# Turned steps spread over places, and side work placed by a table of engine load, in an attention and two-expert-layer kernel

## The chip, the cores and the metric

One core of a Trainium2 chip runs the whole program. The metric is the time on the device in microseconds (us). Three runs of the kernel before took 2199.93 to 2209.55, their median is 2204.12.

## The reference

Block-wise attention gives x (2304 tokens by 512); then comes a layer of 8 experts whose gates P are normalised over rows and columns 8 times; then an MLP with a gated activation.

```python
scores = scale * np.matmul(q_c, k_c.transpose(0, 1, 2, 4, 3))   # chunks of 64
attn = exp(scores - max) / (sum + 1e-09); out = np.matmul(attn, v_c)
...
for e in range(E):                       # 8 experts, 512 -> 1024 -> 512
    h = np.maximum(x @ w1[e], 0.0)
    out += P[:, e:e + 1] * (h @ w2[e])
...
h = x @ w_in                             # 512 -> 2048 -> 512
relu6 = np.clip(h + 3.0, 0.0, 6.0)
return ((h * relu6 / 6.0) @ w_out).astype(np.float32)
```

## The kernel before, in words

All matmuls of the layers work on pairs of operands, a high part in TensorE's reduced 32-bit type and a low part that is the rest: a product is high times high, high times low and low times high. ScalarE makes a high part (a copy), VectorE or GpSimd the low part (a subtraction); `cut_piece` (L789) does both.

The program goes through attention and the first expert (until about 306 us), and then through 108 **steps** (`slots`). A step is one of 36 sets of weights (28 of experts 1 to 7, 4 for each expert, and 8 of the MLP) times one third of the tokens (768). Six passes stand in a row: thirds 0, 1 and 2 with the 28 expert sets (steps 0 to 27, 28 to 55, 56 to 83), then thirds 0, 1 and 2 with the 8 MLP sets (84 to 107). From step 56 on they are called **turned**.

The first layer of a step is a block product with seven multiplications in place of eight (`ORDER`, `product`, L871): six matmuls of 128x384 for each, so 42 a step, into three banks of PSUM a, b and c. The order is 1 into a, 6 into b, 2 onto a, 7 onto b, 5 into c, 4 onto b, 3 onto c. Each of the seven is a **place** of the step. A product that goes onto a bank waits until the bank's first content has been read: ScalarE copies product 1 from a (p1, L916, ahead of product 2), VectorE adds the sums u2, u3 and p1 from b and c (L912).

- In a step of the first two passes `h_first` cuts four outputs, and the second layer of the step before (`mm2_chunk`, L993, 36 matmuls of 128x512) is put between the products.
- In a turned step `h_turned` makes gated outputs (`gate`: for an expert one VectorE instruction with the gate columns `pb`, L942; for the MLP a ScalarE relu, L948, and then a VectorE instruction, L949), and after product 3 four differences (L956) of them, each cut as it is made (`put`). These seven cut outputs are the operands of a second seven-product scheme: `second` takes two steps at a time, one output m of both (`MS` is their order), adds it to `accM` on VectorE (L1101; on ScalarE, L1099, for the first pair of a segment), and in the last pair of a segment adds the blocks to each other (`comb`, L1048, seven times).

Around this there is **side work**, put at (step, place) by `at_slot`: its instructions are issued behind those of the product of that place.

- Conversion (`cv_half`, L188 to L214): the MLP's weights come as 64-bit numbers and are turned into 32-bit ones with seven VectorE instructions for each of 32 pieces, four in one place and three two places later. All lie in the first pass.
- Weights of the expert sets: sums (`w1_sums` L775, `w2_sums` L786, four instructions in one place) and cuts, in the step or two before they are used; all operands are stored to be loaded again in later passes (`w1_load`, asked for two steps ahead).
- Weights of the MLP sets ahead of time (`w1_ahead`, `w2_ahead`): 8 sets in the second pass, 18 places for each; a half (w1 or w2) is cut in four pieces, the low part of w1's on VectorE, and stored whole (`wsc<-m`).
- The input of the MLP (`x2_cuts`): transposed at the end of a segment (`x2_T`), differences and seven cuts for each half.

Every queue runs in the order written; SyncE issues all loads and stores.

Of the kernel before, what the change touches and what calls it, by code (L numbers as in the profile page):

```python
# [9 lines left out]
F32 = mybir.dt.float32  # L10
F32R = mybir.dt.float32r
# [17 lines left out]
def chunk_attention_moe_mlp(  # L29
# [135 lines left out]
    cv_list = W_IN[:8] + W_OUT[:8] + W_IN[8:] + W_OUT[8:]  # L165
    cv_in = {}
    M = {}
# [5 lines left out]
    def cv_load(i):  # L173
        if i < len(cv_list):
            src, _, r, c = cv_list[i]
            t = part(i % 2 * 2 * CW, 2 * CW, U32)
            nc.sync.dma_start(
                out=t,
                in_=src.bitcast(U32)[r * 128:(r + 1) * 128, 2 * c * CW:2 * (c + 1) * CW],
            )  # L180
            cv_in[i] = t

    def cv_half(i, z):
        if z == 0:
            t = cv_in[i].rearrange("p (n a) -> p n a", a=2)
            hw = t[:, :, 1]
            kx = part(4 * CW + i % 2 * CW, CW, U32)
            nc.vector.tensor_scalar(  # L188
                out=kx, in0=hw, scalar1=20, scalar2=0x7FF,
                op0=ALU.logical_shift_right, op1=ALU.bitwise_and,  # L190
            )
            nc.vector.tensor_scalar(
                out=kx, in0=kx, scalar1=-896.0, scalar2=0.0, op0=ALU.add, op1=ALU.max
            )
            nc.vector.tensor_scalar(
                out=kx, in0=kx, scalar1=255.0, scalar2=8388608.0, op0=ALU.min, op1=ALU.mult
            )
            nc.vector.scalar_tensor_tensor(
                out=kx, in0=hw, scalar=0x80000000, in1=kx,
                op0=ALU.bitwise_and, op1=ALU.bitwise_or,  # L200
            )
            cv_in[i] = (t, kx)
            return
        t, kx = cv_in.pop(i)
        am = part(6 * CW, CW, U32)
        nc.vector.tensor_scalar(
            out=am, in0=t[:, :, 1], scalar1=0xFFFFF, scalar2=0x100000,
            op0=ALU.bitwise_and, op1=ALU.bitwise_or,
        )
        bt = part(7 * CW + i % 2 * CW, CW)  # L210
        nc.vector.scalar_tensor_tensor(
            out=bt, in0=t[:, :, 0], scalar=2.0 ** -32, in1=am, op0=ALU.mult, op1=ALU.add
        )
        nc.vector.scalar_tensor_tensor(  # L214
            out=bt, in0=bt, scalar=2.0 ** -20, in1=kx.bitcast(F32), op0=ALU.mult, op1=ALU.mult
        )
        cv_in[i] = bt
        cv_load(i + 2)

    def cv_keep(i):  # L220
        _, dst, r, c = cv_list[i]
        nc.sync.dma_start(
            out=dst[r * 128:(r + 1) * 128, c * CW:(c + 1) * CW], in_=cv_in.pop(i)
        )
# [469 lines left out]
    for seg, (p, mlp, ks) in enumerate(SEGS):  # L694
        for j, kset in enumerate(ks):
            slots.append(SimpleNamespace(
                i=len(slots), seg=seg, p=p, mlp=mlp, k=kset, e=1 + kset // NG4, q=kset % 2, j=j,
                turned=seg >= FIRST_TURNED, H={},
            ))
        ends.append(len(slots))  # L700
# [39 lines left out]
    raw1, raw2 = {}, {}  # L740

# [6 lines left out]

    def raw_load(k):
        s1, _, g = src_of(k)  # L750
        t = pools["raw1"].tile([128, 8, 2, 128], F32, tag="r1", name=f"r1_{k}")
# [7 lines left out]
    def raw_load2(k, ahead=False):  # L759
        _, s2, g = src_of(k)  # L760
        if ahead:
            t = pools["raw1"].tile([128, 8, 256], F32, tag="r1", name=f"r2_{k}")
        else:
            t = pools["raw2"].tile([128, 4, 256], F32, tag="r2", name=f"r2_{k}")
# [6 lines left out]
    def w1_sums(k):  # L771
        t = raw1[k]
        for o, x, y, op in ((4, 0, 1, ALU.add), (5, 4, 2, ALU.subtract), (6, 2, 0, ALU.subtract),
                            (7, 3, 5, ALU.subtract)):
            nc.vector.tensor_tensor(out=t[:, o], in0=t[:, x], in1=t[:, y], op=op)  # L775

    def w2_sums(k):
        r = raw2[k]
        if k < NEXP:
            t = pools["sum2"].tile([128, 4, 256], F32, tag="s2", name=f"s2_{k}")  # L780
        else:
            t = r[:, 4:8]
        A11, A12, A22, A21 = [r[:, o] for o in range(4)]
        for o, x, y, op in ((0, A21, A22, ALU.add), (1, t[:, 0], A11, ALU.subtract),
                            (2, A11, A21, ALU.subtract), (3, A12, t[:, 1], ALU.subtract)):
            nc.vector.tensor_tensor(out=t[:, o], in0=x, in1=y, op=op)  # L786
        raw2[k, "s"] = t
# [52 lines left out]
    def w1_ahead(k, z):  # L840
        w = part(0, 3584, F32R).rearrange("p (o a n) -> p o a n", o=7, a=2)
        if z < 4:
            o0, o1 = PIECES[z]
            r = raw1[k].rearrange("p o k f -> p o (k f)")[:, o0 + 1:o1 + 1]
            cut_ops(w, r, o0, o1, nc.vector)
            return
        raw1.pop(k)
        nc.sync.dma_start(
            out=wsc1[k].rearrange("o p n -> p o n"),
            in_=w.rearrange("p o a n -> p o (a n)").bitcast(F32),  # L850
        )

    def w2_ahead(k, z):
        w = part(0, 3584, F32R).rearrange("p (o a n) -> p o a n", o=7, a=2)
        if z < 4:
            o0, o1 = ((0, 2), (2, 4), (4, 6), (6, 7))[z]
            r = raw2[k, "s"][:, o0:o1] if z < 2 else raw2[k][:, o0 - 4:o1 - 4]
            cut_ops(w, r, o0, o1, nc.gpsimd)
            return
        raw2.pop(k), raw2.pop((k, "s"))  # L860
        w2_store(k, 0, w)
# [34 lines left out]
    def h_first(s, t, pr, ps, z):  # L896

        if pr == 1:
# [39 lines left out]

    def gate(s, out, src, nh):

        if not s.mlp:
            nc.vector.scalar_tensor_tensor(  # L942
                out=out, in0=src, scalar=0.0, in1=pb[s.p, s.e][:, nh * HN:(nh + 1) * HN],
                op0=ALU.max, op1=ALU.mult,
            )
            return
        u = temp(s, "u")
        nc.scalar.activation(out=u, in_=src, func=AF.Relu, bias=three)  # L948
        nc.vector.scalar_tensor_tensor(  # L949
            out=out, in0=u, scalar=6.0, in1=src, op0=ALU.min, op1=ALU.mult  # L950
        )

    def h_turned(s, t, pr, ps, z):

        first_sums(s, t, pr, ps)
        sub = lambda o, x, y: nc.vector.tensor_tensor(out=o, in0=x, in1=y, op=ALU.subtract)  # L956
        if pr == 2:
# [3 lines left out]
        elif pr == 5:  # L961
            gate(s, t["u3"], t["u3"], 1)
            put(s, 3, t["u3"])
        elif pr == 4:
            gate(s, t["p1"], t["p1"], 0)
            put(s, 2, t["p1"])
        elif pr == 3:
            t1, u2, u3, p1 = t["t1"], t["u2"], t["u3"], t["p1"]
            gate(s, u2, u2, 1)
            sub(t1, u2, t1)  # L970
            put(s, 5, t1)
            sub(u2, u3, u2)
            put(s, 7, u2)
            sub(u3, u3, t1)
            put(s, 6, u3)
            sub(p1, p1, u3)
            put(s, 4, p1)
# [41 lines left out]
    MS_LAST = (1, 6, 2, 7, 5, 3, 4)  # L1019
    COMB = {2: [(2, 1)], 5: [(3, 5)], 6: [(6, 1), (7, 6), (3, 6), (5, 7)], 4: [(4, 7)]}  # L1020
    DONE = {2: [2], 6: [3, 5], 4: [4]}
    COMB_LAST = {6: [(6, 1), (3, 6)], 2: [(2, 1)], 7: [(7, 6), (4, 7)], 5: [(3, 5), (5, 7)]}
    DONE_LAST = {2: [2], 5: [5], 3: [3], 4: [4]}
# [129 lines left out]
    def x2_diff(kl):  # L1153
        diffs(*x2t[kl])
# [42 lines left out]
    with tc.manual_schedule():  # L1197
# [140 lines left out]
        def to_right():  # L1338
# [4 lines left out]
            opened("r", "W10", 1, "right")  # L1343
            opened("rr", "raw1", 2, "right")
# [225 lines left out]
```

## Time and profile before

| | us |
|---|---|
| median of 3 runs | 2204.12 |
| the profiled execution | 2206.19 |
| its span, first to last instruction | 2204.3 |
| TensorE busy | 2004.4 |
| VectorE busy | 1425.6 |
| GpSimd busy | 1111.8 |
| ScalarE busy | 801.8 |

The granted clock of TensorE has a mean of 0.967 of full speed. PE is TensorE's matmuls, PEld its weight loads, DVE VectorE, ACT ScalarE, POOL GpSimd, SP SyncE. A busy time counts all of an engine's instructions, whether something waits for them or not; where time is lost is read from idle time and from what ended it.

### The profile page before, as it was taken

To read this page: it belongs to the slowest core of one execution; us is meant where nothing else is said; L and a number is where in the kernel's file an instruction comes from. 1 tells how busy PE (TensorE), PEld (TensorE's weight loads), DVE (VectorE), ACT (ScalarE), POOL (GpSimd) and SP (SyncE) were. 2 spreads that over 40 slices of the span, in tenths; PEclk is the share of its full clock that TensorE was granted. 3 is DMA by queue.
4 is the path that set the end of the run, shared out by engine and by line. 5 is a ranking of instruction groups with operands and counts; after the bars stand their busy time and mean duration, and the time that the engine had idled before them with its cause. 6 is when DMAs were issued, how large, how long until landed. Compare 5 with 4: busy or idle time off the path is not lost.

```text
span 2204.3 us, 33550 instructions
## 1 busy us (share of the span) xinstructions
PE 2004.4 (91%) x11709; PEld 1835.1 (83%) x11709; DVE 1425.6 (65%) x2310; ACT 801.8 (36%) x1586; POOL 1111.8 (50%) x965
## 2 busy tenths in 40 slices
PE   7999989999999999999989988999999877888887
PEld 6777777888888888887878878999999877888887
DVE  6555467787787655556655456777777757656666
ACT  3322234443344344444434423222222333343342
POOL 3213246676667566555555546554545445344343
PEclk9999999999999999999999999999999888999999
DMA  9756486686676779999989968777778777767663
GB/s 213 190 146 175 139 284 228 224 268 206 225 248 226 263 264 328 321 349 350 336 314 329 359 216 303 247 250 248 249 250 284 261 257 242 237 214 245 209 209 124
DMA packets 340935, 552.82 MB, mean 251 GB/s; under 512 B 46736, under 2 KB 170784, under 8 KB 340512
## 3 DMA queue, kind: packets, MB, share of 16 engines
q1 hardware_dynamic: 340768, 550.69, 75.5%
q8 instruction: 93, 1.52, 0.3%
q14 instruction: 74, 0.61, 0.1%
HBM read 365.97 MB, written 184.62 MB: 250 GB/s over the span
## 4 chain that ended last, share of the span: by engine, by line
PE 50%; DVE 25%; DMA 11%; ACT 5%; issue 5%; POOL 2%; SPq 1%; DVEq 0%; ACTq 0%; POOLq 0%
PE acc L993 11%; PE hb L871 9%; PE ha L871 7%; PE hc L871 6%; PE o L1089 5%; PE o L1080 3%; PE h L557 3%; DVE u L956 3%; PE acc L591 3%; DVE p L956 3%; DVE u L912 2%; DMA wsc<-SS 2%; ACT u L948 2%; DMA x2sc<-m 1%; DVE r L775 1%
## 5 line engine op out<-in xcount | busy, mean ns | idle before, releaser
L993 PE MATMUL acc<-W,H 128*128 128x512 f32 x2016 | 526.2, 396 | 5.1 <-POOL H L894 3.0
L993 PEld LDWEIGHTS acc<-W,H 128*128 128x128 f32 x2016 | 380.7, 191 | 66.0 <-POOL H L894 6.8
L871 PE MATMUL hb<-X,W 128*128 128x384 f32 x1560 | 326.5, 345 | 24.9 <-DVE u L912 24.8
L792 POOL TENSOR_TENSOR W<-r,W 128x512 fp32r<-128x512 f32 x220 | 291.8, 1349 | 56.7 <-ACT W L791 53.2
L871 PEld LDWEIGHTS hb<-X,W 128*128 128x128 f32 x1560 | 281.2, 193 | 42.0 <-DVE u L912 32.5
L871 PE MATMUL ha<-X,W 128*128 128x384 f32 x912 | 198.8, 355 | 88.6 <-ACT p L916 74.2
L871 PE MATMUL hc<-X,W 128*128 128x384 f32 x1200 | 245.1, 339 | 14.0 <-DVE H L888 9.8
L871 PEld LDWEIGHTS ha<-X,W 128*128 128x128 f32 x912 | 167.7, 198 | 102.9 <-ACT p L916 79.6
L894 POOL TENSOR_TENSOR H<-u,H 128x384 fp32r<-128x384 f32 x112 | 124.5, 1111 | 229.0 <-ACT H L893 199.9
L871 PEld LDWEIGHTS hc<-X,W 128*128 128x128 f32 x1200 | 212.6, 189 | 27.2 <-DVE H L888 13.5
L912 DVE TENSOR_TENSOR u<-hc,u 128x384 f32<-128x384 f32 x216 | 119.8, 555 | 146.2 <-PE hc L871 142.6
L912 DVE TENSOR_TENSOR u<-hb,p 128x384 f32<-128x384 f32 x216 | 119.7, 554 | 130.7 <-PE hb L871 106.1
L792 POOL TENSOR_TENSOR Hb<-u,Hb 128x384 fp32r<-128x384 f32 x108 | 125.0, 1168 | 126.3 <-ACT Hb L791 102.6
L892 ACT ACTIVATE u<-u 128x384 f32<-128x384 f32 x112 | 58.7, 524 | 292.9 <-DVE u L912 292.7
L1101 DVE SCALAR_TENSOR_TENSOR accM<-o,accM 128x768 f32<-128x768 f32 x154 | 146.1, 950 | 21.9 <-PE o L1089 12.1
L1080 PE MATMUL o<-W2R,Hb 128*128 128x256 f32 x882 | 144.5, 295 | 3.5 <-DVE accM L1101 3.3
L1089 PE MATMUL o<-Hb,W2R 128*128 128x384 f32 x672 | 145.9, 340 | 0.0
L1080 PEld LDWEIGHTS o<-W2R,Hb 128*128 128x128 f32 x882 | 132.2, 203 | 4.0 <-DVE accM L1101 3.5
L791 ACT ACTIVATE W<-r 128x512 fp32r<-128x512 f32 x224 | 122.8, 595 | 1.9 <-DMA r<-in_moe_w_dram 1.9
L1089 PEld LDWEIGHTS o<-Hb,W2R 128*128 128x128 f32 x672 | 121.3, 190 | 0.0
L792 POOL TENSOR_TENSOR Hb<-t,Hb 128x384 fp32r<-128x384 f32 x57 | 67.3, 1180 | 97.8 <-ACT Hb L791 91.2
L1089 PE MATMUL o<-Ha,W2R 128*128 128x384 f32 x504 | 110.8, 338 | 0.0
(190 smaller groups left out, 3585.5 us busy)
## 6 DMA issues: line engine op xcount, KB each, us to landing
W<-wsc SPq DMA_DIRECT2D x504, 256.0 KB, 4.1
W2R<-wsc SPq DMA_DIRECT2D x182, 512.0 KB, 4.3
wsc<-W SPq DMA_DIRECT2D x28, 1792.0 KB, 8.7
r<-in_moe_w_dram SPq DMA_DIRECT2D x112, 256.0 KB, 4.7
wsc<-SS SPq DMA_DIRECT2D x28, 1024.0 KB, 6.3
wsc<-m SPq DMA_DIRECT2D x16, 1792.0 KB, 8.7
wsc<-W SPq DMA_DIRECT2D x28, 768.0 KB, 5.9
x2sc<-m SPq DMA_DIRECT2D x42, 384.0 KB, 5.0
```

The lines of the kernel that those rows point to most:

```text
L557: nc.tensor.matmul(out=hps[:, :n], lhsT=w[:, a, kk, :], rhs=xx[:, kk, :], start=(kk == 0 and a == 0 and xx is xh), stop=(kk == KD - 1 and ...
L591: nc.tensor.matmul(out=o[:, :n] if turned else o, lhsT=w[:, a, c] if turned else hx[:, c], rhs=hx[:, :n] if turned else w[:, a, :], start= ...
L791: nc.scalar.activation(out=hi, in_=r, func=AF.Copy)
L792: lo_eng.tensor_tensor(out=lo, in0=r, in1=hi.bitcast(F32), op=ALU.subtract)
L871: nc.tensor.matmul(out=ps[:, :HN], lhsT=W1t[s.b][:, wo, a, kl, :], rhs=x[:, b, kl, :], start=(start and kl == 0 and a == 0 and b == 0), st ...
L894: nc.gpsimd.tensor_tensor(out=lo, in0=src, in1=hf, op=ALU.subtract)
L912: nc.vector.tensor_tensor(out=o, in0=ps[b][:, :HN], in1=x, op=ALU.add)
L956: sub = lambda o, x, y: nc.vector.tensor_tensor(out=o, in0=x, in1=y, op=ALU.subtract)
L993: nc.tensor.matmul(out=o, lhsT=s.Hs[:, fi, hx, t * 128:(t + 1) * 128], rhs=w[:, 0::3, a, :] if fi == 0 else w[:, 1:3, a, :], start=(s.j % ...
L1080: nc.tensor.matmul(out=o[:, t * 256:(t + 1) * 256], lhsT=hs[q][:, b, t * 128:(t + 1) * 128], rhs=w[:, q, a, :], start=(q, a, b) == mm[0], ...
L1089: nc.tensor.matmul(out=ps[:, d, :HN], lhsT=w[:, q, a, d * 128:(d + 1) * 128], rhs=hs[q][:, b, :], start=(q, a, b) == mm[0], stop=(q, a, b) ...
L1101: nc.vector.scalar_tensor_tensor(out=dst, in0=src, scalar=sc, in1=dst, op0=ALU.mult, op1=ALU.add)
```

## The change

In a turned step the work behind a place is put in another order, and the differences go to places 7, 8, 9 and 11, which are places 0, 1, 2 and 4 of the next step, issued ahead of that step's own work. The relu of the MLP's gate (`squash`) is issued one place ahead of the instruction that uses it. The relu's and the gate's order on each engine is that of the code below.

```diff
+    def h_turned(s, r):
+        t, ps = s.t, s.ps
+        first = lambda pr: first_sums(s, t, pr, ps)
+        if r in (0, 1, 4):
+            first(ORDER[r][0])
+            if r == 4:
+                squash(s, t["u3"])
+        elif r == 2:
+            squash(s, ps["a"][:, :HN])
+        elif r == 3:
+            t["t1"] = temp(s, "t1")
+            gate(s, t["t1"], ps["a"][:, :HN], 0)
+            put(s, 1, t["t1"])
+            first(7)
+        elif r == 5:
             gate(s, t["u3"], t["u3"], 1)
+            first(4)
             put(s, 3, t["u3"])
+            squash(s, t["p1"])
+        elif r == 6:
             gate(s, t["p1"], t["p1"], 0)
+            first(3)
             put(s, 2, t["p1"])
+            squash(s, t["u2"])
+        elif r == 7:
+            gate(s, t["u2"], t["u2"], 1)
+            diff(s, 5, t["t1"], t["u2"], t["t1"])
+        elif r == 8:
+            diff(s, 7, t["u2"], t["u3"], t["u2"])
+        elif r == 9:
+            diff(s, 6, t["u3"], t["u3"], t["t1"])
+        elif r == 11:
+            diff(s, 4, t["p1"], t["p1"], t["u3"])
...
                 product(s, pr, s.ps[b], start)
+                if prev is not None and prev.turned:
+                    h_turned(prev, z + 7)
+                (h_turned if s.turned else h_first)(s, z)
```

Side work is divided into single instructions or cuts (`cv_op`, `w1_sum`, `w2_sum`, `ahead_cut`, `x2_diff`), and each is put by `book` at the first place from a given one at which a table of planned load has room. The table is filled first with the steps' own work (0.56 for a sum or gate, 0.53 and 1.05 for a cut, 0.75 and 0.96 for the additions to acc and accM).

```diff
+        load = {e: [0.0] * (7 * (len(slots) + 2)) for e in ("DVE", "ACT", "POOL")}
+        CAP = {"DVE": 1.95, "ACT": 2.4, "POOL": 2.6}
...
+    CV_COST = (0.45, 0.43, 0.45, 1.08, 0.49, 0.72, 0.8)
...
+        def book(g, fn, *a, dve=0.0, act=0.0, pool=0.0):
+            need = (("DVE", dve), ("ACT", act), ("POOL", pool))
+            def full(e, c):
+                v = load[e]
+                if g < 7 * TURN + 7:
+                    return v[g] + c > CAP[e]
+                return max(sum(v[g - 2:g + 1]), sum(v[g - 1:g + 2]), sum(v[g:g + 3])) + c > 6.0
+
+            while any(c and full(e, c) for e, c in need):
+                g += 1
+            use(g, dve, act, pool)
+            at_slot(0, g, fn, *a)
+            return g
...
+        CV1 = 25
+        g = book_cv(12, list(range(CV1)), True)
...
+        book_cv(g0, list(range(CV1, len(cv_list))), False)
...
+        g = book_ahead(g0, range(NEXP, FAR), 2, 2)
+        g = book_ahead(done[1] + 8, range(FAR, NSET), 1, 2)
```

By it 25 conversions stay in the first pass and 7 go to the second; of the 8 MLP sets 4 stay in the second pass and 4 (`FAR` on) go to the third, where raw weights come into one buffer of the tile M in place of two of their own. The table, worked through, puts the first four sets into steps 38 to 48 and the others into steps 65 to 82, and the side work on the last third's MLP input into steps 86 to 98.

The cut pieces go into two buffers in turn, all low parts are GpSimd's, and each piece is stored by itself, two places after its cut:

```diff
+        WA["n"] = n = WA.get("n", 0) + 1
+        w = part(5 * CW + n % 2 * 1024, 1024, F32R).rearrange("p (o a n) -> p o a n", o=2, a=2)
...
+        cut_piece(w[:, :, 0], w[:, :, 1], r, nc.gpsimd)
...
+                        g = book(g, ahead_cut, kset, m, z, z == order[3], act=c, pool=1.8 * c)
+                        at_slot(0, g + 2, ahead_keep, kset, m, z)
+                        g += step
```

The gate columns' pool is opened earlier, so that the columns of the first turned step are asked for two steps ahead (before: at the end of the step before). The order of outputs in the very last pair becomes 1, 2, 3, 6, 7, 5, 4 (before: 1, 6, 2, 7, 5, 3, 4).

## Rows read from the trace of the kernel before

**Rows 1.** The page, section 1: busy us, share, instructions.
```profile
PE 2004.4 (91%) x11709; PEld 1835.1 (83%) x11709; DVE 1425.6 (65%) x2310; ACT 801.8 (36%) x1586; POOL 1111.8 (50%) x965
```

**Rows 2.** Stretches, products' line L871 alone: start:end, length, PE, PEld, clock, DMA, GB/s.
```profile
339.10:774.00 434.90, 221.99 (x1093) 194.47 (x1094) 1.00 0.69 234
692.70:708.30 15.60, 8.39 (x43) 7.55 (x43) 1.00 0.75 264
774.00:1266.30 492.30, 241.34 (x1177) 213.12 (x1176) 0.97 0.93 327
982.10:1053.00 70.90, 34.48 (x171) 30.09 (x170) 0.98 0.99 354
1266.30:1359.80 93.50, 45.44 (x212) 39.88 (x211) 0.93 0.76 257
1359.80:1727.00 367.20, 205.35 (x1008) 176.00 (x1009) 1.00 0.79 262
1727.00:1884.00 157.00, 69.53 (x294) 57.87 (x295) 0.86 0.72 247
1884.00:2161.20 277.20, 136.39 (x630) 112.33 (x631) 0.95 0.66 212
1997.20:2013.70 16.50, 8.65 (x42) 7.08 (x43) 1.00 0.64 215
2161.20:2204.30 43.10, 8.65 (x42) 6.99 (x42) 0.92 0.41 130
```

**Rows 3.** Waits of PE, 339.1 to 774.0: total us, times, longest.
```profile
PE ha L871 <- DVE p L912: 13.8, 12, 2.7
```

**Rows 4.** Waits of PE, 774.0 to 1266.3.
```profile
PE hb L871 <- DVE u L912: 17.2, 9, 4.7
```

**Rows 5.** Waits of PE, 1266.3 to 1359.8.
```profile
PE ha L871 <- ACT p L916: 8.0, 3, 3.3
PE x L1128 <- DVE m L1133: 3.7, 1, 3.7
PE hc L871 <- DVE t L942: 3.6, 1, 3.6
```

**Rows 6.** Waits of PE, 1359.8 to 1727.0.
```profile
PE ha L871 <- ACT p L916: 8.4, 24, 0.8
```

**Rows 7.** Waits of PE, 1727.0 to 2161.2.
```profile
PE ha L871 <- ACT p L916: 70.1, 22, 6.7
```

**Rows 8.** Timeline of an MLP step's end: start, us, engine, instruction, idle before.
```profile
1996.56 0.55 DVE L912 TENSOR_TENSOR u<-hc,u 128x384 f32<-128x384 f32 x1
...
1998.87 0.56 DVE L956 TENSOR_TENSOR t<-u,t 128x384 f32<-128x384 f32 x1
...
1999.53 0.53 ACT L791 ACTIVATE Hb<-t 128x384 fp32r<-128x384 f32 x1 [1.71 <-DVE t L956]
...
2000.79 1.19 DVE L956 TENSOR_TENSOR p<-p,u 128x384 f32<-128x384 f32 x1
...
2001.90 0.95 DVE L1101 SCALAR_TENSOR_TENSOR accM<-o,accM 128x768 f32<-128x768 f32 x1
...
2002.50 0.47 ACT L916 ACTIVATE p<-ha 128x384 f32<-128x384 f32 x1
...
2003.03 1.31 PE L871 MATMUL ha<-X,W 128*128 128x384 f32 x6 [1.42 <-ACT p L916]
```

**Rows 9.** Timeline around a segment's last pair, 1919 to 1932.
```profile
1919.46 4.29 DVE L1048 TENSOR_TENSOR accM<-accM 128x768 f32<-128x768 f32 x4
...
1931.86 2.29 PE L871 MATMUL ha<-X,W 128*128 128x384 f32 x6 [5.69 <-ACT p L916]
```

**Rows 10.** Groups of DVE, 339.1 to 774.0: busy us, mean ns, idle before.
```profile
L198 DVE SCALAR_TENSOR_TENSOR m<-m 128x512 uint32<-128x512 uint32 x30 | 35.1, 1171 | 1.0
```

**Rows 11.** Groups of DVE, 774.0 to 1266.3.
```profile
L792 DVE TENSOR_TENSOR m<-r,m 128x512 fp32r<-128x512 f32 (+1 forms) x32 | 32.9, 1027 | 31.6 <-ACT m L791 31.6
```

**Rows 12.** DMA issues by line: engine, count, KB each, median us to landing.
```profile
wsc<-m SPq DMA_DIRECT2D x16, 1792.0 KB, 8.7
```

More of the change, by code (lines that the diff above doesn't have):

```diff
@@ L164, in chunk_attention_moe_mlp @@
     W_OUT = [(w_out, scr_out, r, c) for r in range(FD2 // 128) for c in range(DM // CW)]
-    cv_list = W_IN[:8] + W_OUT[:8] + W_IN[8:] + W_OUT[8:]
+    cv_list = W_IN[:8] + W_OUT[:8] + W_IN[8:] + [W_OUT[r] for z in range(8, 12) for r in (z, z + 4)]
     cv_in = {}
@@ L222, in cv_keep @@
         nc.sync.dma_start(
-            out=dst[r * 128:(r + 1) * 128, c * CW:(c + 1) * CW], in_=cv_in.pop(i)
+            out=dst[r * 128:(r + 1) * 128, c * CW:(c + 1) * CW], in_=part(4 * CW, CW)
         )
@@ L740, in chunk_attention_moe_mlp @@
     raw1, raw2 = {}, {}
+    FAR = NEXP + NG4
     def src_of(k):
@@ new lines, in chunk_attention_moe_mlp, with use @@
+        CAP = {"DVE": 1.95, "ACT": 2.4, "POOL": 2.6}
+        def use(g, dve=0.0, act=0.0, pool=0.0):
+            for e, c in (("DVE", dve), ("ACT", act), ("POOL", pool)):
+                load[e][g] += c
+        for s in slots:
+            g = 7 * s.i
+            if not s.turned:
+                for z in range(7):
+                    use(g + z, dve=0.56 * (z > 0), act=(0.5, 0, 0.5, 0, 1.1, 1.1, 1.1)[z],
+                        pool=1.05 * (z > 3))
+                if s.j % NG4 == NG4 - 1:
+                    for z in range(TP):
+                        use(g + 7 + z, dve=0.75)
+                continue
+            relu = 0.6 * s.mlp
+            for r, (d, a, h) in {0: (0, 0.5, 0), 1: (1, 0, 0), 2: (0, relu, 0), 3: (2, 0, 1),
+                                 4: (1, relu, 0), 5: (2, relu, 1), 6: (2, relu, 1), 7: (2, 0, 1),
+                                 8: (1, 0, 1), 9: (1, 0, 1), 11: (1, 0, 1)}.items():
+                use(g + r, dve=0.56 * d, act=a + 0.53 * h, pool=1.05 * h)
+            if s.i >= TURN + 2:
+                for z in range((s.i - TURN) % 2 == 0, 7, 2):
+                    use(g + z, dve=0.96)
@@ new lines, in book_cuts @@
+        def book_cuts(g, end, pieces):
+            for fn, *a in pieces:
+                small = a[-1] == 3 and fn is w1_piece
+                g = book(g, fn, *a, act=0.4 if small else 0.62, pool=0.7 if small else 1.3)
+            assert g < end, (g, end, pieces)
+            return g
+        for s in slots[:NEXP]:
+            if s.i > 1:
+                g = 7 * (s.i - 2) + 3
+                for n in range(4):
+                    g = book(g, w1_sum, s.k, n, dve=0.43)
+            if s.i == 1:
+                for z in range(4):
+                    at_slot(0, z, w1_piece, s, z, nc.vector)
+                at_slot(0, 6, w1_keep, s)
+            elif s.i:
+                g = book_cuts(max(g + 1, 7 * (s.i - 1)), 7 * s.i,
+                              [(w1_piece, s, z) for z in range(4)])
+                at_slot(0, g + 2, w1_keep, s)
+            if s.i and s.i + 2 < NEXP:
+                at_slot(s.i - 1, 4, raw_load, s.k + 2)
```

325 lines of the change are left out of this document (167 added, 158 removed).

## The prediction

> **What bounds the kernel now.** First the page: TensorE is busy for 91% of the span [rows 1], so the question is where the other tenth is lost. Then the table of stretches for the products' line [rows 2], which tells steps apart, since a step has 42 of these matmuls. A step of the first two passes that nothing disturbs takes 15.6 us (692.7 to 708.3, clock 1.00). The 26 steps from 339.1 take 434.9, which is 29.3 over 26 clean ones; the 28 from 774.0 take 492.3, 55.5 over. In the turned passes the 24 steps from 1359.8 take 367.2, or 15.3 each. An MLP step with nothing beside it (1997.2 to 2013.7) takes 16.5 with a wait of 1.42 in it [rows 2, 8], so 15.1 clean; the 7 steps from 1727.0 are 51.3 over that and the 15 from 1884.0 are 50.7 over. These excesses come to 187 us, and the granted clock tells the same: 0.86 in the worst stretch, 1.00 in the clean ones.
>
> Third, who ended TensorE's waits. In the first two passes it is VectorE's partial sums: 13.8 us for sum p alone in the one [rows 3], 17.2 for sum u in the other [rows 4]. From 1359.8 on it is almost only ScalarE's copy of the first product (L916): 8.4 us in the expert part [rows 6] and 70.1 in the MLP part [rows 7]. The chain of that wait stands in the timeline of one step's end [rows 8]: the last sum starts at 1996.56, three differences follow the gate before the fourth (p) starts at 2000.79, its high part must be cut on ScalarE, and only then, at 2002.50, the copy runs that the third product waits for until 2003.03. VectorE's order is the cause: all four differences stand in a row.
>
> **The staging of turned steps.** After the last sum, relu and gate, only one difference and its cut remain ahead of the copy. In that same timeline the cut of the first difference starts at 1999.53 and the copy could follow at about 2000.1, so it runs 2.4 us earlier; the wait there was 1.42 [rows 8]. The 1.0 left over takes in one more VectorE instruction of the second product (0.95, L1101) in the steps where it falls between. So a plain turned step loses its wait: 8.4 us in the expert part. The other three differences go to places 8, 9 and 11, beside later products, and their work is the same.
>
> The seven additions at a segment's end are not moved except in the last group. Four of them hold VectorE for 4.29 us and the step after waits 5.69 [rows 9]. The three differences that leave that chain are worth 0.56, 0.56 and 1.19 [rows 8], so some 3.4 stays, with a slower clock after it and 1 us in the step before: I leave 6.5 us of each segment end's some 14 (the two steps' excess).
>
> **Stretch by stretch.**
> - 0 to 339.1: attention, the first expert and the two first steps are placed as before but for later conversions: 0 (0 to 5 gained).
> - 339.1 to 774.0: conversions go one operation at a time and 25 of 32 stay here. One half now issues four in a row, of which the dearest takes 1.17 [rows 10]; three that the table lets into one place take less than 3.6 with a sum's 0.55 beside them, within two products of TensorE's time. I take 21 of 29.3 (bounds 0 and 29).
> - 774.0 to 1266.3: 32 low parts leave VectorE for GpSimd; with their waits for ScalarE they held it 32.9 + 31.6 us [rows 11]. Four of the eight sets of MLP weights move behind 1266.3, and seven conversions come in. Against that stands memory traffic: 0.93 share at 327 GB/s, and 354 GB/s at share 0.99 in a part of it [rows 2]. 327 times 492.3 is 161 MB; four sets less (4.7 MB each by the diff's sizes) and seven conversions more (0.8 each) make 148 MB, 417 us at 354 GB/s, which fits. But worked through, the table puts the remaining four sets and the conversions into 11 steps, with some 6.4 MB each: 18.1 us at 354 GB/s against 15.6. That is 27 us that stay, and I take 29 of 55.5 (bounds 0 and 53).
> - 1266.3 to 1359.8: the wait of 3.6 for the gate columns goes, since they are asked for two steps ahead; the 8.0 for the copy falls to 2; the 3.7 for the transposed input halves as VectorE has fewer differences before it [rows 5]; the clock, now 0.93, gives 2 more. 14 (bounds 4 and 20).
> - 1359.8 to 1727.0: 8 from the staging, less 10 for the four sets that come in. Each set is cut in 8 pieces into two buffers. A piece is stored two places after its cut and its buffer is taken again two places later, 4.3 us here, where the store of a whole set's half (seven pieces of operands) lands after 8.7 [rows 12]; a piece is two sevenths of it. If a third of the 32 pieces wait 1 us before the copy, that is 10. Net 2 lost (bounds 40 lost and 8 gained).
> - 1727.0 to 1884.0: of 51.3 over, 6.5 stays for the segment's end and 5 for the side work on the last third, which the table spreads over 12 steps in place of 6. 40 (bounds 15 and 48).
> - 1884.0 to 2161.2: two segment ends at 6.5 and 0.3 in each other step stay of 50.7. 33 (bounds 10 and 48).
> - The end: 43.1 us for one step, then a second product that VectorE's additions pace. Staging lets its first instruction run some 4 us earlier, and the order of the last group changes little. 5 (bounds 0 and 8).
>
> Sum: 21 + 29 + 14 - 2 + 40 + 33 + 5 = 140. The profiled execution took 2206.19 (span 2204.3 and 1.9 around it), so 2066; the median of the three runs is 2204.12, 2.1 lower, which makes 2064.
>
> Queues: SyncE gets 64 stores of pieces for 16 of halves, and two ahead of each place's weight loads; a store whose piece is late holds the loads behind it, but these are asked for two steps, some 30 us, before their product, so I cost it at nothing; without that cover it costs what the cut is late. GpSimd gets the 32 low parts at about 1.2 us, 38 us in 11 steps, beside a load with room for it, since its outputs there are stored and not multiplied. The later start of the differences makes their halves late by up to four places, and the second product of that half (m=4) is six places away.
>
> **Rivals.** (1) **VectorE becomes the bound in turned steps.** The fourth difference takes 1.19 where the first takes 0.56 [rows 8], and GpSimd is at work on a low part in that time. Spread out, every gate and difference (eight in an MLP step) meets one. Eight at 1.19, five sums at 0.55 and 3.5 second-product additions at 0.95 make 15.6 a step, over the 15.1 of TensorE. The MLP stretches would then keep 0.7 in each of 22 steps and more wherever side work comes, some 28 us, and the expert part 8: 2100. Against it: the first and third differences ran at 0.56 next to ScalarE's work, and a place has room. The Trainium skill, page SBUF — State Buffer, section Who interferes with whom, says that a VectorE instruction with both inputs in SBUF contends with a GpSimd instruction that reads SBUF, and that whichever issues later is blocked for the whole of the other; by that rule this rival is the forecast, and the trace agrees for the fourth difference (1.19) and not for the first (0.56).
> (2) **Memory is not tight.** Loads run two steps ahead, so a backlog of 27 us is never felt: 16 more from 774.0 and 9 more from 1359.8: 2039. For it: no row names a weight load as the end of a wait.
> (3) **The stores of pieces hold ScalarE, and it is slower.** If a piece lands after 8.7 us like the half before it [rows 12] and not after 4.3, each of 64 cuts waits 4.4 on ScalarE with the copy behind it: 280 us against 140 gained, 2344. It decides from where a piece lands 2.2 us late, 6.5 in all. Against it: a piece carries two sevenths of the bytes.
> (4) **The table's prices are too low.** It has 1.08 for the operation that takes 1.17 [rows 10] and nothing for the additions at a segment's end; VectorE still jams and half of the gain is lost: 2134.
>
> **How the numbers follow.** Forecast 0.55, rival 1 0.18, rival 2 0.15, rival 3 0.06, rival 4 0.06. The range, 2015 to 2125, holds the forecast and rivals 1 and 2 with the bounds of their costs, and leaves out rivals 3 and 4. Half a percent, 11 us, is about what a measurement of this kernel can tell from no change. Faster by more 0.92, slower by more 0.06 (rival 3), and 0.02 between, for smaller forms of rival 3.
>
> **What would show it.** In the new profile: TensorE's wait for L916 in the MLP part under 25 us in place of 70, most of it in the step after a segment's end; clean steps of 15.1 between; the gate columns' wait gone at the first turned step; waits for VectorE's sums under 10 us in the second pass; share of DMA 0.95 or more where the four sets lie. Rival 1 would show as VectorE near 0.95 busy in MLP steps and the two-input operations at 1.1 and more; rival 3 as ScalarE waiting for the stores of pieces. A time over 2150 would mean that the order on ScalarE or VectorE, not the four differences, set the step.

## The result, and the profile after

The changed kernel takes 2016.65 us (median of four runs, 2011.85 to 2019.33) against 2206.28 for four runs of the one before: a ratio of 0.914, with a 95% interval of 0.911 to 0.917. The forecast was 2064 in a range of 2015 to 2125, so the time lies inside by only 1.65 us: two of the four runs lie under 2015, and so does the median of five later runs (2014.52). The gain is some 190 us where the sum had 140.

The page of the changed kernel, first line and section 1, answers to [rows 1]:

```profile
span 2009.8 us, 33618 instructions
PE 1942.4 (97%) x11709; PEld 1800.9 (90%) x11709; DVE 1389.0 (69%) x2278; ACT 795.6 (40%) x1586; POOL 1147.3 (57%) x997
```

TensorE does the same 11709 matmuls; its share rose from 91% to 97%, since the span shrank by more than its busy time. That busy time fell by 62 us. In the same profiles the mean granted clock rose from 0.967 to 0.989 and fewer groups start behind a wait; how the 62 us divide between the two was not measured. The same stretches as in [rows 2], cut at the same steps, for the products' line alone (start:end, length, PE, PEld, clock, DMA share, GB/s):

```profile
333.50:738.80 405.30, 217.52 (x1094) 195.20 (x1093) 1.00 0.74 237
738.80:1198.10 459.30, 234.63 (x1177) 209.31 (x1177) 1.00 0.94 326
897.80:1087.10 189.30, 92.56 (x463) 81.76 (x462) 1.00 1.01 359
1198.10:1269.50 71.40, 41.72 (x212) 36.76 (x211) 1.00 0.81 279
1269.50:1622.30 352.80, 202.98 (x1008) 177.22 (x1009) 1.00 0.95 331
1622.30:1732.10 109.80, 60.67 (x294) 50.36 (x295) 0.98 0.88 302
1732.10:1972.90 240.80, 131.85 (x630) 108.83 (x631) 0.98 0.81 272
1972.90:2009.80 36.90, 8.55 (x42) 6.99 (x42) 0.93 0.46 152
```

| steps | before | after | gained | forecast |
|---|---|---|---|---|
| 0 to 1, and all before them | 339.1 | 333.5 | 5.6 | 0 |
| 2 to 27, first pass | 434.9 | 405.3 | 29.6 | 21 |
| 28 to 55, second pass | 492.3 | 459.3 | 33.0 | 29 |
| 56 to 60, first turned steps | 93.5 | 71.4 | 22.1 | 14 |
| 61 to 84, expert part | 367.2 | 352.8 | 14.4 | -2 |
| 85 to 91 | 157.0 | 109.8 | 47.2 | 40 |
| 92 to 106 | 277.2 | 240.8 | 36.4 | 33 |
| 107 and the end | 43.1 | 36.9 | 6.2 | 5 |

(The gains add up to 194.5, the difference of the two profiled spans; the forecasts to 140.) The first pass now runs at the 15.6 us of a clean step throughout (405.3 for 26). What is left stands mainly in two places, and TensorE's waits name them (us in total, times, longest us). From 738.8 to 1198.1:

```profile
PE hc L871 <- DVE H L888: 8.1, 7, 2.8
PE acc L1011 <- POOL H L894: 7.2, 5, 2.8
```

And from 1622.3 to 1972.9, the line that answers to [rows 7], where it was 70.1:

```profile
PE ha L871 <- ACT p L917: 14.7, 5, 5.3
```

At the head of a plain MLP step nothing waits any more. The timeline of the same place as [rows 8], in another step (start, us, engine, instruction, idle before):

```profile
1929.51 0.56 DVE L994 TENSOR_TENSOR t<-u,t 128x384 f32<-128x384 f32 x1
1930.10 0.53 ACT L787 ACTIVATE Ha<-t 128x384 fp32r<-128x384 f32 x1 [0.59 <-DVE t L994]
...
1930.53 0.47 ACT L917 ACTIVATE p<-ha 128x384 f32<-128x384 f32 x1
...
1932.62 1.22 PE L871 MATMUL ha<-X,W 128*128 128x384 f32 x6
...
1937.92 0.55 DVE L994 TENSOR_TENSOR p<-p,u 128x384 f32<-128x384 f32 x1
```

One difference and one cut stand ahead of the copy; it ends 1.6 us before the third product comes for it. The last difference starts 7.4 us after the copy, beside other products.

### The profile page after: what moved, and what is told of

Same layout as the page of the kernel before. It is cut to its first block, busy times and chain, and to the rows that moved or that the text cites. A ratio compares the mean times of both kernels' runs of the same rounds, so it can differ in the third digit from the quotient of the medians.

```text
span 2009.8 us, 33618 instructions
## 1 busy us (share of the span) xinstructions
PE 1942.4 (97%) x11709; PEld 1800.9 (90%) x11709; DVE 1389.0 (69%) x2278; ACT 795.6 (40%) x1586; POOL 1147.3 (57%) x997
## 4 chain that ended last, share of the span: by engine, by line
PE 79%; DMA 7%; DVE 7%; POOL 3%; issue 2%; SPq 2%; ACT 2%; DVEq 0%; ACTq 0%; POOLq 0%
PE acc L1011 19%; PE hb L871 15%; PE ha L871 10%; PE o L1107 10%; PE hc L871 10%; PE o L1098 7%; PE h L546 3%; PE acc L580 3%; DMA wsc<-m 2%; DVE accM L1066 1%; POOL SS L788 1%; DMA q_None<-in_q_dram 1%; DVE accM L1119 1%; SPq L259 1%; DMA r<-in_moe_w_dram 1%
## 5 line engine op out<-in xcount | busy, mean ns | idle before, releaser
L1011 PE MATMUL acc<-W,H 128*128 128x512 f32 x2016 | 519.1, 392 | 10.0 <-POOL H L894 7.2
L1011 PEld LDWEIGHTS acc<-W,H 128*128 128x128 f32 x2016 | 376.0, 188 | 68.0 <-POOL H L894 9.8
L871 PE MATMUL hb<-X,W 128*128 128x384 f32 x1560 | 319.2, 339 | 0.9 <-DVE u L913 0.6
L871 PEld LDWEIGHTS hb<-X,W 128*128 128x128 f32 x1560 | 276.8, 189 | 13.3 <-DVE u L913 2.2
L871 PE MATMUL hc<-X,W 128*128 128x384 f32 x1200 | 243.6, 338 | 9.5 <-DVE H L888 8.9
L871 PEld LDWEIGHTS hc<-X,W 128*128 128x128 f32 x1200 | 211.5, 188 | 22.0 <-DVE H L888 12.2
L871 PE MATMUL ha<-X,W 128*128 128x384 f32 x912 | 188.2, 341 | 15.4 <-ACT p L917 14.7
L871 PEld LDWEIGHTS ha<-X,W 128*128 128x128 f32 x912 | 161.9, 190 | 21.9 <-ACT p L917 16.2
L1107 PE MATMUL o<-Hb,W2R 128*128 128x384 f32 x660 | 141.5, 337 | 0.2 <-DMA W2R<-wsc 0.2
L788 POOL TENSOR_TENSOR Hb<-u,Hb 128x384 fp32r<-128x384 f32 x93 | 103.4, 1113 | 59.4 <-ACT Hb L787 49.0
L1098 PE MATMUL o<-W2R,Hb 128*128 128x256 f32 x846 | 130.8, 285 | 0.0
L1098 PEld LDWEIGHTS o<-W2R,Hb 128*128 128x128 f32 x846 | 119.3, 192 | 0.1
L546 PE MATMUL h<-xh,w 128*128 128x256 f32 (+1 forms) x384 | 108.5, 349 | 0.0
```

What stands on the lines that cost most here:

```text
L546: nc.tensor.matmul(out=hps[:, :n], lhsT=w[:, a, kk, :], rhs=xx[:, kk, :], start=(kk == 0 and a == 0 and xx is xh), stop=(kk == KD - 1 and ...
L788: lo_eng.tensor_tensor(out=lo, in0=r, in1=hi.bitcast(F32), op=ALU.subtract)
L871: nc.tensor.matmul(out=ps[:, :HN], lhsT=W1t[s.b][:, wo, a, kl, :], rhs=x[:, b, kl, :], start=(start and kl == 0 and a == 0 and b == 0), st ...
L1011: nc.tensor.matmul(out=o, lhsT=s.Hs[:, fi, hx, t * 128:(t + 1) * 128], rhs=w[:, 0::3, a, :] if fi == 0 else w[:, 1:3, a, :], start=(s.j % ...
L1098: nc.tensor.matmul(out=o[:, t * 256:(t + 1) * 256], lhsT=hs[q][:, b, t * 128:(t + 1) * 128], rhs=w[:, q, a, :], start=(q, a, b) == mm[0], ...
L1107: nc.tensor.matmul(out=ps[:, d, :HN], lhsT=w[:, q, a, d * 128:(d + 1) * 128], rhs=hs[q][:, b, :], start=(q, a, b) == mm[0], stop=(q, a, b) ...
```

## The experiments

### The two halves of the change, each alone

Where no number of runs is given, a kernel of this section ran once. Stretches of a profile are steadier than whole times: steps 2 to 27 took 405.3 us in all nine profiles whose first pass is as in the change. Steps 85 to 106 are less so, with 345.8 to 351.8 in the eight profiles that have them as in the change.

The new order of turned steps put into the kernel before (`h_turned`, `squash`, `diff` and the order of the last pair as in the change, all side work as it was):

```diff
+                if prev is not None and prev.turned:
+                    h_turned(prev, z + 7)
+                (h_turned if s.turned else h_first)(s, z)
```

> The kernel before with the new order of a turned step alone (relu a place ahead, differences at places 7, 8, 9 and 11, new order of the last pair); all side work placed as before. If the four differences ahead of the copy set the turned step, the time from the first turned step to the end falls from 938.0 us of before (811.6 of after) to 835, within 15, the first 56 steps keep their 960, and the whole comes to about 2100. If the placement of side work carries the turned part, it stays above 890 there and 2150 in all.

Measured: 2098.38 us beside 2199.80 for the kernel before. Its stretches of steps 2 to 27, 28 to 55, 61 to 84 and 56 to the end, in this order:

```profile
338.10:770.50 432.40, 221.05 (x1093) 193.51 (x1094) 1.00 0.70 236
770.50:1263.70 493.20, 241.66 (x1177) 213.57 (x1176) 0.97 0.93 327
1350.60:1702.80 352.20, 202.70 (x1009) 177.45 (x1009) 1.00 0.83 272
1263.70:2095.90 832.20, 448.63 (x2186) 382.49 (x2184) 0.98 0.81 268
```

And the table's placement with a turned step in the old order:

```diff
+        elif pr == 3:
             squash(s, t["u2"])
-        elif r == 7:
             gate(s, t["u2"], t["u2"], 1)
             diff(s, 5, t["t1"], t["u2"], t["t1"])
-        elif r == 8:
             diff(s, 7, t["u2"], t["u3"], t["u2"])
-        elif r == 9:
             diff(s, 6, t["u3"], t["u3"], t["t1"])
-        elif r == 11:
             diff(s, 4, t["p1"], t["p1"], t["u3"])
```

> The changed kernel with a turned step's work in the old order (relu beside its gate, four differences in a row behind the last product); all side work stays where the table put it. If the differences set the turned step, the wait for L917 at its head is back, 0.3 in an expert step and 1.4 in an MLP step and more at the three segment ends: 870 to 885 us from the first turned step to the end (811.6 in the changed kernel), about 2075 in all, and the first 56 steps stay at 897. If the placement carries it, under 835 there.

Measured: 2121.92 us. The stretches of steps 61 to 84, and of 56 to the end:

```profile
1283.40:1658.40 375.00, 205.40 (x1009) 176.02 (x1009) 1.00 0.90 311
1197.90:2119.90 922.00, 461.92 (x2186) 390.10 (x2184) 0.96 0.76 261
```

TensorE's largest wait in the second of them (in total, times, longest):

```profile
PE ha L871 <- ACT p L917: 87.8, 50, 5.8
```

The first 56 steps gain from the placement alone (1266.3 to 1197.9; staging leaves them at 1263.7), and the turned part from the staging: 938.0 to 832.2 with it alone, 922.0 without it, 811.7 with both. So of the 126 us gained there, 106 to 110 are the staging's, and 16 to 20 the placement's. The 922 came out above the 885 expected: the wait for the copy stayed as long as it was before (87.8 us in 50 waits, against 8.0, 8.4 and 70.1 of [rows 5], [rows 6] and [rows 7]), and the expert part became slower than before (375.0 against 367.2), as did the steps from 92 to 106 (283.1 against 277.2). That the expert part paid for the four sets' pieces which the table puts there fits the 7.8 us, since with the new order the same sets cost it 0.6 (352.8 with them, 352.2 without).

The two together: 2199.80 less 101.4 less 77.9 is 2020.5, and the change is 2016.65, so in total they hardly interact. In single stretches they do: the expert part is one, the first turned steps are another (6.6 and 8.0 us alone, 22.1 together).

### What in the placement helps the first pass

The 25 conversions of the first pass put back into bursts of four and three:

```diff
-                    g = book(g, cv_op, i, x, dve=c)
+                    use(g + (0 if x < 4 else 2), dve=c)
+                    at_slot(0, g + (0 if x < 4 else 2), cv_op, i, x)
...
+                g += 7
```

> The changed kernel with the 25 conversions of the first pass in bursts again: four operations in one place and three two places later, one piece each 7 places; the same 25. If bursts on VectorE cause the waits of the first pass, steps 2 to 27 take 425 us or more (434.9 before, 405.3 after). If it is the number of conversions there (32 before, 25 now), they take 412 or less.

And all 32 there, at the places of the kernel before, with the weights' sums left where the table has them:

```diff
-        CV1 = 25
-        g = book_cv(12, list(range(CV1)), True)
+        CV1 = 32
...
+        for i in range(len(cv_list)):
+            o = 23 * i // 4
+            for x in range(7):
+                at_slot(0, 6 + o + 2 * (x > 3), cv_op, i, x)
...
```

> The changed kernel with all 32 conversions in the first pass again, in the bursts and at the places of the kernel before; the sums and cuts of weights stay where the table puts them. If the number of conversions (25 or 32) decides the first pass, steps 2 to 27 go from 405.3 back to 425 us or more (434.9 before). If it is the sums of weights, one to a place where four stood in one, they take 412 or less.

Measured: 2013.40 and 2024.72 us. The stretch of steps 2 to 27 of the one with bursts:

```profile
336.80:743.60 406.80, 218.22 (x1094) 193.89 (x1093) 1.00 0.74 236
```

Steps 2 to 27 and 28 to 55 of the one with all 32:

```profile
337.80:769.10 431.30, 220.98 (x1094) 193.30 (x1093) 1.00 0.72 235
769.10:1214.00 444.90, 234.15 (x1178) 209.85 (x1177) 1.00 0.93 324
```

Bursts cost 1.5 us. Thirty-two conversions, one every 5.75 places and not every 7, and in bursts, cost 26.0, which is 24.5 more than 25 in bursts and nearly all of the 29.6 that the first pass gained. TensorE's largest waits in those 431.3 us are again those for VectorE's sums (8.2 us for sum p, 5.2 for u):

```profile
PE ha L871 <- DVE p L913: 8.2, 7, 1.8
```

So what counted is how much VectorE has to do beside a step, and with 25 conversions the order within it did not matter. Thirty-two without bursts were not run. The bill comes in the second pass: without the seven that moved there it takes 444.9 and not 459.3. So moving them gains 26.0 and costs 14.4.

### The gate columns of the first turned step

The load asked for at the end of the step before again, at the place of the kernel before:

```diff
-            at_slot(i - 2, 2, pb_load, 2, e)
+            at_slot(*((i - 2, 2) if i > TURN else (TURN - 1, 6)), pb_load, 2, e)
```

> The changed kernel with the gate columns of the first turned step asked for at the end of the step before, as before. If their landing (9 to 13 us) held VectorE there, steps 56 to 60 take 75 to 79 us (93.5 before, 71.4 after) with a wait of some 3.6 for the sum or gate that needs them. If the staging hides it, since the gate now stands at place 3, no more than 72.

Measured: 2017.01 us, and 72.0 for steps 56 to 60. VectorE waits 1.3 us for the load, TensorE 0.3. But the load was not as late here as it was before: it was issued 4.3 us ahead of step 56, and 0.1 us ahead in the kernel before. The staging alone, which keeps the old time of asking (0.1 us ahead, landing 13.4 us later), shows what that costs. VectorE and then TensorE wait in its first turned step:

```profile
DVE t L953 <- DMA pb<-ptd: 5.0, 1, 5.0
PE hc L871 <- DVE t L953: 4.0, 1, 4.0
```

So the new order does not hide a load as late as before. Asking for it earlier is what removes the wait, and 4.3 us ahead of the step do nearly as well as two steps.

### Where the second pass still loses 17.8 us

In steps 38 to 48 (897.8 to 1087.1) the table has four sets and seven conversions, 189.3 us for 11 steps of 15.59 (405.3 / 26). ScalarE's waits in the second pass of the changed kernel have this line for the cuts of pieces:

```profile
ACT m L787 <- DMA wsc<-m: 60.2, 19, 7.9
```

Each cut writes into a buffer that has to be stored first. The 23 pieces of 512 KB there land 5.8 us (median) after their issue, where the forecast allowed 4.3.

The longest of these waits can be followed to TensorE in the timeline. ScalarE waits 7.91 us for a store, its next high part (L887) is late by that, VectorE's low part (L888) waits for that, and TensorE's next product onto bank c waits for VectorE:

```profile
990.11 0.63 ACT L787 ACTIVATE m<-r 128x512 fp32r<-128x512 f32 x1 [7.91 <-DMA wsc<-m]
991.68 0.47 ACT L887 ACTIVATE H<-ha 128x384 fp32r<-128x384 f32 x1
992.19 0.56 DVE L888 SCALAR_TENSOR_TENSOR H<-ha,H 128x384 fp32r<-128x384 f32 x1 [4.85 <-ACT H L887]
992.80 1.34 PE L871 MATMUL hc<-X,W 128*128 128x384 f32 x6 [2.80 <-DVE H L888]
```

Three kernels bear on it, all built on the changed one; each differs by one line. They cut the pieces three places apart and not two, store each piece one place after its cut and not two, and put six sets and not four into the second pass:

```diff
-        g = book_ahead(g0, range(NEXP, FAR), 2, 2)
+        g = book_ahead(g0, range(NEXP, FAR), 2, 3)
...
-                        at_slot(0, g + 2, ahead_keep, kset, m, z)
+                        at_slot(0, g + (1 if bufs > 1 else 2), ahead_keep, kset, m, z)
...
-    FAR = NEXP + NG4
+    FAR = NEXP + 6
```

> The changed kernel with the pieces of the four sets in the second pass three places apart and not two, so they reach over some 15 steps and not 11. In steps 38 to 48 ScalarE waits 60 us for the stores of pieces and TensorE loses 17.8 us. If the traffic (359 GB/s at a share of 1.0) or the two buffers cause that, the second pass takes 12 to 18 us less than 459.4 and the whole about 2002. If the additional work itself (cuts on ScalarE and GpSimd) causes it, under 5 less.

> The changed kernel with the pieces of the second pass stored one place after their cut and not two; the same bytes, but each buffer has 2.2 us more until it is taken again. If ScalarE's wait for a buffer is the cause, its waits for these stores fall from 60 us to 20 to 35 and the second pass takes 6 to 12 us less than 459.4. If the bytes are the cause, the waits move to another place and it takes within 3 us of 459.4.

> The changed kernel with six MLP sets in the second pass and two in the third (four and four). If the pieces' stores and two buffers cost TensorE 17.8 us for four sets (steps 38 to 48), each set more there costs 4 to 5: the second pass takes 466 to 471 us (459.3), and the third pass is not faster than 353, since four sets cost nothing there. If only the conversions beside them make the traffic too much, the two sets more are free: within 3 us of 459.3.

Measured: 1998.11 us (four runs; 0.907 of the kernel before, 0.903 to 0.911), 2007.30 and 2017.10. The second pass and steps 38 to 48 of the kernel with pieces three places apart:

```profile
742.90:1187.90 445.00, 234.42 (x1177) 209.49 (x1176) 1.00 0.97 336
901.90:1078.50 176.60, 92.37 (x463) 81.97 (x462) 1.00 1.01 364
```

The second pass and steps 38 to 48 of the one that stores each piece a place earlier:

```profile
740.80:1192.20 451.40, 235.44 (x1178) 210.63 (x1177) 1.00 0.95 332
899.80:1082.80 183.00, 93.39 (x464) 83.12 (x463) 0.99 1.03 376
```

And of the one with six sets:

```profile
744.10:1207.60 463.50, 236.03 (x1179) 210.41 (x1178) 0.99 0.98 342
```

Three places apart: 14.3 us less, and ScalarE's wait falls from 60.2 to 4.8. This run alone can't tell buffers from bytes: length times GB/s gives 64.3 MB for its steps 38 to 48 where the change moved 68.0, and both run at 359 to 364 GB/s. The second kernel tells them apart: storing a place earlier leaves the bytes in these steps (68.8 MB), and they take 183.0 us at 376 GB/s, so 359 was not the limit. The second pass takes 7.9 us less, and ScalarE's wait falls to 35.3.

The buffers need company, though. With all 32 conversions back in the first pass (above), the pieces have the same two buffers and the same two places, and ScalarE still waits 44.9 us for their stores, at most 4.9 at once. Yet steps 38 to 48 take 176.5 us, as with pieces three places apart:

```profile
928.10:1104.60 176.50, 92.09 (x464) 82.30 (x463) 1.00 1.01 359
```

So the loss needs both, the short time until a buffer is taken again and the seven conversions beside it. Whether these act through their bytes (63.4 MB here) or through VectorE is open. Two more sets cost 4.2 us, near 2 each and not 4 to 5, though ScalarE then waits 80.2 us in all; the runs don't split that further.

### The relu a place ahead

Each relu put right before its gate again:

```diff
-        elif r == 2:
-            squash(s, ps["a"][:, :HN])
...
+            squash(s, t["u3"])
             gate(s, t["u3"], t["u3"], 1)
```

> The changed kernel with the relu of an MLP gate issued right before the gate that uses it, in the same place, and the differences still at places 7, 8, 9 and 11. If the differences alone set the MLP step, steps 85 to 106 stay within 6 us of 350.6. If VectorE's waits for the relu count too (0.74 us each, four a step), they take 358 to 380.

Measured: 2015.95 us, and 353.3 for steps 85 to 106 (350.6 in the profile of the changed kernel, 348.1 in its second, 345.8 to 351.8 in all eight profiles of these steps as in the change). So of the staging it is the differences that count; what the relu's place is worth is hardly clear of that spread.

### The segment's end, and the best version

In the changed kernel the three steps after a segment's last pair still wait 3.5, 5.35 and 3.5 us. This kernel puts the block additions one to a place, up to four places later (the last pair of all is left), with pieces three places apart as above:

```diff
+    LATE = {2: [(2, (2, 1), 2)], 5: [(1, (3, 5), 0)],
+            6: [(1, (6, 1), 0), (2, (3, 6), 3), (3, (7, 6), 0), (4, (5, 7), 5)],
+            4: [(3, (4, 7), 4)]}
...
                     second(n, y)
+                    for g, pair, x in late.pop(14 * n + y, ()):
+                        comb(*pair)
+                        if x:
+                            block_out(g, x)
```

> The changed kernel as it is, for the comparison with the three that run beside it: 2010 to 2020 us. If the 5 us that the attention part was shorter in the profile of after come from the run and not from the change, its first step starts anywhere from 300 to 307 us.

> The changed kernel with pieces three places apart in the second pass, and with the block additions at a segment's end one to a place (up to five places later) where four stood in one place. The three steps after the last pairs lose 5.0, 6.8 and 5.1 us over 15.1. If the row of four additions causes that, the MLP part takes 10 to 15 us less and the whole comes to about 1990. If the work on the last third's MLP input causes it, 4 us or less from this, and about 2000.

Measured on the same chip: 2014.52 us for the changed kernel (five runs; its first step starts at 306.6 in the profile) and 1985.19 for this one (five runs, 1983.66 to 1988.58; 0.901 of the kernel before, 0.898 to 0.904). The row of four additions and the wait behind it, from the timeline of the changed kernel:

```profile
1765.31 3.90 DVE L1066 TENSOR_TENSOR accM<-accM 128x768 f32<-128x768 f32 x4
1776.43 2.29 PE L871 MATMUL ha<-X,W 128*128 128x384 f32 x6 [5.35 <-ACT p L917]
```

The stretch of steps 85 to 106 of the kernel with the later additions:

```profile
1609.80:1946.40 336.60, 189.56 (x925) 157.12 (x925) 0.99 0.85 293
```

What remains there of TensorE's wait for the copy:

```profile
PE ha L871 <- ACT p L917: 6.1, 5, 2.3
```

The kernel with pieces three places apart, which lacks only the later additions, has 345.8 us there, so they are worth 9.2; against the two profiles of the change it is 14.0 and 11.5. The steps after the last pairs fall from 20.1, 21.9 and 20.1 us to 16.0, 18.8 and 15.9: the row of four was the larger part of what they lost, and not all of it. With 1985.19 this is the fastest version, 29 us ahead of the change.

The fifth wait of the MLP part has another cause. Step 92 takes 18.7 us in the changed kernel and still 16.8 in this one. There ScalarE waits for the store of a cut piece of the MLP's input, and the copy stands behind that cut:

```profile
1737.28 0.52 ACT L634 ACTIVATE m<-m 128x384 fp32r<-128x384 f32 x1 [2.80 <-DMA x2sc<-m]
1738.12 0.47 ACT L917 ACTIVATE p<-ha 128x384 f32<-128x384 f32 x1
```

TensorE's product then waits 2.11 us for the copy. With the side work placed as before (staging alone) step 92 takes 14.8.

## Why the prediction was right, and where its terms were off

**The bound.** The bottleneck was read correctly: TensorE's waits for the copy behind four differences, and for VectorE's sums. The two halves alone confirm both: the placement acts on the first 56 steps, and 106 of the 126 us of the turned ones go to the staging. The size was less well forecast. The sum fell some 50 us short of the gain, every term of it was too low, and the time lies inside the range by 1.65 us; that it lies inside at all owes as much to a wide range as to the terms, and is in part luck.

**Staging.** The mechanism is confirmed, and "8.4 us in the expert part" was too small. With the staging alone these 24 steps take 352.2, 15.0 less. Before, and with the staging alone (start:end, length, then busy us of PE, PEld, DVE, ACT and POOL, clock, DMA share, GB/s):

```profile
1359.80:1727.00 367.20, 358.78 (x2018) 351.03 (x2017) 267.41 (x396) 99.61 (x196) 186.21 (x170) 1.00 0.79 262
1350.60:1702.80 352.20, 352.20 (x2018) 352.20 (x2017) 251.26 (x397) 98.16 (x196) 181.68 (x169) 1.00 0.83 272
```

The 8.4 us of waits went, and TensorE's busy time for the same 2018 matmuls fell by another 6.6, which the sum had at nothing. So a step's length less its wait was too long for a clean step: 14.7 us here, and 14.8 in the MLP part where the forecast had 15.1. In the MLP part the chain was predicted 2.4 us shorter; the profile has the copy end 1.6 us before it is needed where it was 1.42 late [rows 8].

**Segment ends.** "I leave 6.5 us of each": steps 86, 94 and 102 of the changed kernel take 20.1, 21.9 and 20.1 us, so 5 to 7 stayed. That term was right, and the last run shows the larger part of its cause.

**First pass, 21 against 29.6.** The reason given was wrong: "conversions go one operation at a time" is worth 1.5 us. That 25 stay of 32 is worth 24.5 to 26.0; the forecast named it in the same sentence and gave it no price of its own.

**Second pass, 29 against 33.0.** "27 us that stay" were worked out from memory at 354 GB/s; 17.8 stayed, in the steps named, at 359 GB/s. But TensorE's waits there come from rival 3's chain, stores of pieces that hold ScalarE. As a limit by bytes the term fails, since as many bytes went through the same steps in 183.0 us at 376 GB/s when each was stored a place earlier. Rival 2, that memory is not felt, holds for weight loads alone: TensorE's waits for them come to 0.2 us in the MLP part and do not show in the second pass. The other reason given, that 32 low parts leave VectorE, was tested by no run, so how the 33.0 divide is open.

**First turned steps, 14 against 22.1.** The term for the gate columns was right in its reason: without the earlier asking the staging alone still waits 4.0 us for them. The sum was too small because the halves need each other here. Staging alone brings these five steps from 93.5 to 86.9 and leaves waits of 7.8 for the copy and 4.0 for the gate. Placement alone brings them to 85.5 and leaves 6.7 for the copy and 3.7 for the transposed input. Both together make 71.4, with 0.9 us of waits.

**Third pass, -2 against +14.4.** The largest miss, and the one step that failed as a mechanism: the 10 us charged for four sets' pieces. With them the expert part takes 352.8, with the staging and without them 352.2: 0.6 us, at a DMA share of 0.95. A raw buffer is single there, so pieces come more slowly (17.5 steps for four sets and not 11), and ScalarE waits only 2.6 us in all for `wsc<-m`. The charge let each wait of ScalarE pass on to TensorE through the copy, but the staging gives that copy time to spare (1.6 us in the MLP step shown above). In the old order, without that time, the expert part with the same sets is 7.8 us longer than without (375.0 against 367.2). The rest of the miss, 7.0, is the staging's term above.

**85 to the end, 78 against 89.8.** Side work was priced at 5 and 4.7 us. Most steps between the segment ends run at 14.8 or 14.9, under the 15.1 taken for clean, and a few at 15.3 to 15.9. The side work shows most in step 92 (18.7), by a wait that the forecast did not have.

**Attention, 0 against 5.6.** Here nothing failed: the first step begins at 301.2 in the profile of after and between 302.7 and 309.0 in the other twelve, all of them with the same attention part (before 306.5, the change profiled again 306.6). It belongs to the run.

**Rivals.** Rival 1, VectorE as the bound, did not come, though its premise is partly there. VectorE is busy for 291.44 of the 352.8 us of the expert part, 83%, and TensorE waits for none of it there. The four differences now take:

```profile
L994 DVE TENSOR_TENSOR u<-u,t 128x384 f32<-128x384 f32 x24 | 21.3, 889 | 0.0
L994 DVE TENSOR_TENSOR t<-u,t 128x384 f32<-128x384 f32 x24 | 21.0, 875 | 2.5
L994 DVE TENSOR_TENSOR u<-u,u 128x384 f32<-128x384 f32 x24 | 18.9, 788 | 0.3
L994 DVE TENSOR_TENSOR p<-p,u 128x384 f32<-128x384 f32 x24 | 17.6, 732 | 0.0
```

That is 3.3 us a step where three at 0.56 and one at 1.19 made 2.9. The Trainium skill (SBUF — State Buffer, Who interferes with whom) lets such an instruction be blocked by a GpSimd instruction that reads SBUF; the trace agrees: of these 96 differences the 51 that start while a GpSimd instruction runs take 1.06 us on average, and the other 45 take 0.55. So the rival had the mechanism and not the price, 1.19 for each: about half of them meet nothing. The prediction's reading that the first difference of [rows 8] speaks against it was wrong, because GpSimd was idle when that one ran (1998.87 to 1999.43), between the two instructions below. The third difference started together with the second of them, and there it was GpSimd's that took longer, 1.43 against 1.02:

```profile
1997.33 1.02 POOL L792 TENSOR_TENSOR Ha<-p,Ha 128x384 fp32r<-128x384 f32 x1 [1.67 <-issue]
2000.13 1.43 POOL L792 TENSOR_TENSOR Hb<-t,Hb 128x384 fp32r<-128x384 f32 x1 [1.77 <-ACT Hb L791]
```

Rival 3 came in kind, in steps 38 to 48 and in step 92, and not in size. Rival 4, prices too low, did not come for the conversions: even in bursts 25 of them held the first pass to 406.8.

## What to carry to other kernels

Look first for the instruction at the head of a step that stands in an in-order queue behind work nobody needs yet, and move that work behind it; here this was 106 of 190 us, with the same 2310 VectorE instructions. When side work is spread, price how much of it a stretch gets rather than how finely it is cut, and follow each buffer that is stored and taken again. With two places from the store to the next use ScalarE waited 60 us here, with three 35, with four (pieces three places apart) 5. A full DMA queue cost TensorE time here where an engine with other work behind it waited for a landing. And before charging a delay to the bottleneck, see how much time to spare the same change gives on the way to it.

## What the runs showed that was not expected

DMA engines at a share of 1.01 and 364 GB/s for 176 us slowed TensorE by only 5 us (steps 38 to 48 with pieces three places apart, 176.6 against 171.5), with weight loads asked for two steps ahead.

The granted clock fell after a short wait and not after a longer one. In the changed kernel a wait of 2.11 us is followed by six matmuls in 2.29 us, at a granted clock of 0.51, the 1.2 GHz level. One of 2.80 is followed by six in 1.34, at 1.00, the 2.4 GHz level. TensorE was busy throughout the 5 us and more before each wait. The row at 992.80 stands above, with the stores; the other is this:

```profile
1738.64 2.29 PE L871 MATMUL ha<-X,W 128*128 128x384 f32 x6 [2.11 <-ACT p L917]
```

The stretches of the two groups (the last three numbers are granted clock, DMA share and GB/s):

```profile
1738.60:1740.90 2.30, 2.26 (x7) 2.26 (x8) 2.28 (x3) 0.41 (x1) 2.22 (x3) 0.51 1.05 391
992.80:994.20 1.40, 1.40 (x7) 1.37 (x8) 1.40 (x2) 1.02 (x2) 1.40 (x2) 1.00 0.93 358
```

So a price for a stall's after-effect is an average at best: here the slowed stretch came after the shorter wait.
